# Windowed attention with sinks, then RWKV channel mix: the sink tokens' rows of v come by four small transfers instead of a selection matmul per sequence, with new engine choices, order and buffers

## The chip, the cores and the metric

The kernel runs on one core of one Trainium2 chip. The metric is the device time of one execution in microseconds (us); the figure for the kernel before is the median of 3 runs, 165.95 us (165.86 to 165.98). In the profile the engines are PE (matrix products), PEld (loading of PE's weights), DVE (VectorE), ACT (ScalarE), POOL (GpSimd) and SP (SyncE, which here only issues transfers). SPq, POOLq and the like are the instruction queues of these engines. "L676" is line 676 of the kernel before; in the kernel after, the same code stands 10 to 13 lines further down (L808 is L819 there, L939 is L950, and so on).

## The reference

Two layers follow each other. The first is attention in which each position sees the 4 first positions of its sequence (the sinks) and the last 128 positions. B = 4 sequences, H = 8 heads, S = 768 positions, D = 64:

```python
scores = scale * np.matmul(q, k.transpose(0, 1, 3, 2))
keep = is_sink | in_window            # pos < 4, or 0 <= i - j < 128
a = softmax(where(keep, scores, -1e9))
x = matmul(a, v)                      # then heads side by side: [B, S, 512]
```

The second is the RWKV channel mix over the 512 columns of x, with 1024 hidden columns:

```python
xk = mu_k * x + (1.0 - mu_k) * x_prev      # x_prev: one position earlier
xr = mu_r * x + (1.0 - mu_r) * x_prev
k = np.maximum(xk @ w_k, 0.0)
out = sigmoid(xr @ w_r) * (k * k @ w_v)
```

All inputs and the output are fp32; the kernel computes its products in bf16.

## The kernel before, in words

**Tiling.** The work is cut into 12 units: 4 sequences of 3 blocks with 256 positions each, unit u being block u mod 3 of sequence u div 3. A unit passes through four functions, and PE works on several units at a time.

- `prepare` loads q, k and v of the unit on SP (fp32), casts them to bf16 (L536 or L543 for q and k, L646 for v) and turns q and k so that the head dimension lies on the partitions. Where PE does this, it takes four transposes into a PSUM bank (L576) and a copy out (L589). For k of units 4 to 11 and q of units 8 to 11 SP issues DMA transposes instead (L562); such a transpose stands in SP's queue between loads and stores.
- `attend` computes the transposed scores (L721), their exponential (ACT, L775), the mask (DVE, L789; units 0 and 1 get it as a bias from products with an identity, L728), and the products with v (L808). A column of ones beside v gives the sum of the weights, so L822 takes its reciprocal and L825 multiplies. For the blocks 1 and 2 of a sequence the sinks are outside the window's blocks: their scores are products of `ksink` and q (L696), exponentiated (L703), and their share of the result is the product with `vsink` (L763).
- `mix` brings x into the layout with columns on the partitions (PE L849 with a copy L858; for units 9 to 11 DMA transposes from SP, L869), then DVE makes the difference td to the previous position (L877) and from it xk and xr (L888, four instructions of half a unit's width each).
- `ffn` runs one unit behind: the key products (L939, 32 per unit, xk by w_k), relu (L949 on ACT, L953 on DVE), square (L963 on DVE, L967 on ACT), the gate's products (L979, xr by w_r) and tanh (L985), the value products (L997), the final product with the gate (L1006) and the store (L1013). The last half of the last unit is done in two parts (`last_product`, L909, L919, L924).

**The sinks' operands.** Once per sequence, from its first block. `ksink` holds for each pair of heads c a group of 32 columns, in which head a of the pair has its four sinks' keys at columns 4a to 4a + 3; the rest is zero. Two copies on POOL fill it from kt (L670). `vsink` has the matching rows: partition 32c + 4a + i holds row i of v for head 2c + a, in this head's columns and nowhere else. To get rows 0 to 3 of v to these partitions, PE multiplies the bf16 v of the block with `spread`, a 0/1 matrix that picks them (L676, 512 columns into a bank), and DVE multiplies the bank by the 0/1 matrix `hmask` into `vsink` (L680). There are two `ksink` and two `vsink`, used by turns.

**What sets the order.** The whole program is written as a list of operations (`P.op`), each with an engine, a cost for a planner, what it reads and writes, and the pool from which it takes a buffer. The finished plan stands in the file as three tables: `CHOICE` gives the engine of operations that may run on several (casts, copies, relu, square), `SLOTS` the buffer that each operation takes, `ORDER` the sequence in which the operations are emitted. Each engine executes its instructions in that order, and waits at an instruction until the results it needs are there and its buffer is free. A negative number in `ORDER` is a fill: a product with zeros into a bank (L1018), during the start. Within POOL's and SP's queues transfers are issued in the same way, in order. PSUM has 8 banks: two pairs for scores (`sc`) and four for all else (`bank`); the operand bank of L676 is one of these four.

The constants are made by POOL at the start: `ident` and `hmask` (L418), `spread` (L451), the masks, and the column of ones of `vsink` (L470).

## Time and profile before

| | |
|---|---|
| median of 3 runs | 165.95 us (165.86 to 165.98) |
| span of the profiled execution | 164.3 us, so 1.65 us below the median |
| PE busy | 158.4 us (96%), 1603 matmuls |
| DVE busy | 145.4 us (89%), 381 instructions |
| ACT busy | 131.2 us (80%), 218 instructions |
| POOL busy | 13.5 us (8%), 38 instructions |
| data moved | 34.6 MB, 211 GB/s on average |

The span runs from the first to the last record of the profiled execution; a run's time also has what lies around it. A row of the timeline has its start, its length, its engine, its line and operation, the tile written and the tile read, and the number of instructions that follow each other; in square brackets stand the idle time of the engine before it and what ended that. The chain of waits is followed back from the last instruction: each row is what the next one waited for, or the instruction before it on the same engine. A row of the windows has the stretch, its length, and then for PE, weight loads, DVE, ACT and POOL the busy time with the number of instructions, PE's granted clock (1.00 is the full one), the share of the time in which DMA engines moved data, and GB/s. A row that groups instructions has their number, their busy time and mean length in ns, and the idle time before them with what ended it; the row of a tile has the shortest, median and longest length in ns and the first and last start.

### The profile page before, as it was taken

How to read it: one execution, taken by the hardware profiler on the slowest of the kernel's cores; microseconds unless marked ns; L12 is line 12 of the kernel's file. 1: busy time of each engine (PE TensorE's matmuls, PEld its weight loads, DVE VectorE, ACT ScalarE, POOL GpSimd, SP SyncE). 2: the span in 40 equal slices, each digit the busy share in tenths (PEclk: the TensorE clock that was granted, in tenths of full speed). 3: DMA queues.
4: the chain of work that ended last, by engine and by line, in shares of the span. 5: the costliest groups of instructions: out<-in, count | busy, mean ns of one | idle time of the engine just before them, and what ended most of it. 6: DMA issues, size and time to landing. Idle time of an engine off the chain costs nothing.

```text
span 164.3 us, 4195 instructions
## 1 busy us (share of the span) xinstructions
PE 158.4 (96%) x1603; PEld 102.6 (62%) x1603; DVE 145.4 (89%) x381; ACT 131.2 (80%) x218; POOL 13.5 (8%) x38
## 2 busy tenths in 40 slices
PE   6999889999999999999999999999999999999992
PEld 2455568866467587577566775856575765664851
DVE  5259999999999999989999999999999999789752
ACT  3277999999999999999999999997668759163240
POOL 6409300010000000060000000000000000000000
PEclk9999999999999999999999999999999999999999
DMA  4999999999969896999999887986996955077743
GB/s 120 247 305 311 348 335 355 301 354 210 228 154 270 135 240 148 234 198 167 224 216 157 188 156 163 235 146 150 199 123 136 362 149 200 0 90 297 262 185 128
DMA packets 79042, 34.60 MB, mean 211 GB/s; under 512 B 67112, under 2 KB 73520, under 8 KB 79024
## 3 DMA queue, kind: packets, MB, share of 16 engines
q1 hardware_dynamic: 79008, 34.35, 86.3%
q8 instruction: 12, 0.20, 0.6%
q14 instruction: 6, 0.05, 0.1%
q10 hardware_dynamic: 16, 0.00, 0.0%
HBM read 24.12 MB, written 6.29 MB: 185 GB/s over the span
## 4 chain that ended last, share of the span: by engine, by line
PE 79%; ACT 8%; SPq 4%; DMA 3%; issue 2%; DVE 1%; POOL 1%; DVEq 0%; ACTq 0%; POOLq 0%
PE bank L997 23%; PE bank L939 23%; PE bank L979 12%; PE bank L808 6%; PE sc L721 6%; SPq L337 3%; DMA qs<-in_q_dram 3%; PE bank L576 2%; ACT e L775 2%; PE bank L849 2%; ACT rl L949 1%; PE bank L763 1%; ACT qt L589 1%; PE bank L909 1%; PE bank L1018 1%
## 5 line engine op out<-in xcount | busy, mean ns | idle before, releaser
L775 ACT ACTIVATE e<-sc 128x1024 bf16<-128x1024 f32 (+1 forms) x48 | 46.1, 994 | 1.8 <-PE sc L721 1.7
L939 PE MATMUL bank<-xk,wk_sb 128*128 128x256 bf16 x384 | 47.1, 273 | 0.0
L997 PE MATMUL bank<-wv_h,kk 128*128 128x512 bf16 x184 | 43.1, 379 | 0.1
L939 PEld LDWEIGHTS <-wk_sb 128*128 128x128 bf16 x384 | 36.4, 98 | 7.4 <-issue 0.4
L949 ACT ACTIVATE rl<-bank 128x512 bf16<-128x512 f32 x40 | 24.2, 625 | 8.6 <-PE bank L939 7.1
L997 PEld LDWEIGHTS <-kk 128*128 128x128 bf16 x184 | 17.1, 98 | 17.8 <-issue 0.4
L789 DVE TENSOR_TENSOR e<-e,mask 128x1024 bf16<-128x1024 bf16 (+1 forms) x40 | 25.4, 642 | 0.7 <-ACT e L775 0.5
L979 PE MATMUL bank<-wr_sb,xr 128*128 128x512 bf16 x96 | 23.7, 379 | 0.0
L888 DVE SCALAR_TENSOR_TENSOR xk<-td,mu_all,xt 128x256 bf16<-128x256 bf16 x48 | 22.4, 483 | 0.3
L888 DVE SCALAR_TENSOR_TENSOR xr<-td,mu_all,xt 128x256 bf16<-128x256 bf16 x48 | 22.1, 475 | 0.2
L967 ACT ACTIVATE kk<-rl 128x512 bf16<-128x512 bf16 x29 | 18.3, 664 | 4.2 <-DVE rl L953 4.0
L985 ACT ACTIVATE th<-bank 128x512 f32<-128x512 f32 x24 | 15.1, 646 | 5.7 <-PE bank L979 5.7
L825 DVE TENSOR_TENSOR x<-bank,rec 128x256 bf16<-128x256 f32 x48 | 19.2, 416 | 0.4
L808 PE MATMUL bank<-vb,e 128*128 128x65 bf16 x352 | 16.6, 194 | 0.0
L1006 DVE SCALAR_TENSOR_TENSOR w<-th,bank 128x512 f32<-128x512 f32 x19 | 13.0, 682 | 3.6 <-issue 1.8
L808 PEld LDWEIGHTS <-e 128*128 128x128 bf16 x352 | 13.6, 97 | 3.5
L979 PEld LDWEIGHTS <-xr 128*128 128x128 bf16 x96 | 8.8, 98 | 8.6 <-issue 0.2
L721 PE MATMUL sc<-qt,kt 64*128 64x128 bf16 (+1 forms) x256 | 13.9, 238 | 0.0
L721 PEld LDWEIGHTS <-kt 64*128 64x128 bf16 x256 | 8.9, 94 | 5.7 <-issue 3.1
L1018 PE MATMUL bank<-warm 128*128 128x512 bf16 x30 | 10.6, 484 | 1.1 <-DVE warm L1038 1.1
L877 DVE TENSOR_TENSOR td<-xt 128x512 bf16<-128x512 bf16 x24 | 10.3, 428 | 0.7 <-ACT xt L858 0.5
L589 ACT COPY qt<-bank 128x512 bf16<-128x512 bf16 x15 | 9.4, 643 | 1.0 <-PE bank L576 1.0
(74 smaller groups left out, 161.7 us busy)
## 6 DMA issues: line engine op xcount, KB each, us to landing
ks<-in_k_dram SPq DMA_DIRECT2D x24, 256.0 KB, 4.7
qs<-in_q_dram SPq DMA_DIRECT2D x24, 256.0 KB, 4.4
vs<-in_v_dram SPq DMA_DIRECT2D x24, 256.0 KB, 4.4
out_dram<-w SPq DMA_DIRECT2D x19, 256.0 KB, 2.7
w<-in_moe_w_k_dram SPq DMA_DIRECT2D x2, 1024.0 KB, 10.4
w<-in_moe_w_v_dram SPq DMA_DIRECT2D x2, 1024.0 KB, 9.3
w<-in_moe_w_r_dram SPq DMA_DIRECT2D x1, 1024.0 KB, 9.7
out_dram<-ob SPq DMA_DIRECT2D x4, 256.0 KB, 2.6
```

Source lines behind the costliest of these rows:

```text
L721: nc.tensor.matmul(out=sc[:, a, o0:o1], lhsT=lhs[rows], rhs=rhs[rows], start=u not in BIAS, stop=True, skip_group_check=u in BIAS)
L775: nc.scalar.activation(out=buf[ek][:, :, lo:], in_=buf[sck][:, :, lo:], func=AF.Exp, scale=scale)
L789: nc.vector.tensor_tensor(out=at, in0=at, in1=m, op=ALU.mult)
L808: nc.tensor.matmul(out=o[:, g, a, :], lhsT=e[:, a, e0:e0 + 128], rhs=rhs, start=(T == 0 and i == 0), stop=(i == len(blocks) - 1), skip_gro ...
L825: P.op("DVE", dve(256), lambda ok=ok, rk=rk, c=c: nc.vector.tensor_tensor(out=buf["x", u][:, :, 128 * c:128 * c + 128].rearrange("p g (a d ...
L888: nc.vector.scalar_tensor_tensor(out=buf[key][:, c, :], in0=buf[tk][:, i, :], scalar=mu[w][:, c:c + 1], in1=xt[:, c, t0 - 1:t0 + 255], op0 ...
L939: nc.tensor.matmul(out=ps[:, i, :], lhsT=wk_sb[:, c, 128 * f:128 * f + 128], rhs=xk[:, c, :], start=(c == 0), stop=(c == NC - 1), skip_gro ...
L949: nc.scalar.activation(out=buf[rk], in_=buf[psk].rearrange("p (i t) -> p i t", i=2), func=AF.Relu)
L967: nc.scalar.activation(out=buf["kk", u][:, 2 * f2:2 * f2 + 2, :], in_=buf[rk], func=AF.Square)
L979: nc.tensor.matmul(out=buf[psk], lhsT=buf["xr", u][:, c, 128 * g:128 * g + 128], rhs=wr_sb[:, c, :], start=(c == 0), stop=(c == NC - 1))
L985: P.op("ACT", act(512), lambda psk=psk, tk=tk: nc.scalar.activation(out=buf[tk], in_=buf[psk], func=AF.Tanh, scale=0.5), rank + 4 + g, tak ...
L997: nc.tensor.matmul(out=buf[psk], rhs=wv_h[:, f, :], lhsT=buf["kk", u][:, f, 128 * g:128 * g + 128], start=(f == 0), stop=(f == NF - 1))
```

## The change

**The sinks' rows of v.** A new fp32 tile `vstage` [128, 4, 64] is cleared with the other zeros. Four transfers issued by POOL (L491 of the kernel after) fill its partitions i, 16 + i, 32 + i, ... (one of each 16) with row i of v: partition 16h + i gets row i of head h, for all four sequences. The sinks of head h therefore stand at 16h to 16h + 3 rather than at 32c + 4a; the copies into `ksink` (L680 after) and `hmask` are moved to the same places. `vsink` of a sequence is then one product, `vstage` of that sequence (the same for all eight heads) by `hmask` (L686 after). It reads no bank, and may stand on POOL or DVE. The selection matmul, its bank, `spread` and its constants are gone.

```diff
@@ tiles and constants
-    spread = tile1([128, 128], BF16, "spread")
+    vstage = tile1([128, B, D], FP32, "vstage")
...
-        for t, value in ((ones, 1.0), (spread, 0.0), (hmask, 1.0)):
+        for t, value in ((ones, 1.0), (hmask, 1.0)):
...
-        for t in ksink + vsink:
+        for t in ksink + vsink + [vstage]:
             nc.vector.memset(t, 0.0)
...
-    def make_spread():
-        for a in range(2):
-            nc.gpsimd.tensor_copy(
-                out=spread[0:NS, :].rearrange("p (c w) -> p c w", w=32)[:, :, 4 * a:4 * a + NS],
-                in_=ident[0:NS, 0:NS].unsqueeze(1).to_broadcast([NS, NP, NS]))
...
-            keep(m, -4 * a, [[-32, NP], [0, D + 1]], 1, m)
-            keep(m, 3 + 4 * a, [[32, NP], [0, D + 1]], -1, m)
+            keep(m, -16 * a, [[-32, NP], [0, D + 1]], 1, m)
+            keep(m, 3 + 16 * a, [[32, NP], [0, D + 1]], -1, m)
...
+    for i in range(NS):
+        P.op("POOL", 1000.0, lambda i=i: nc.gpsimd.dma_start(
+            out=vstage[i::16], in_=v[:, :, i, :].rearrange("b h d -> h b d")), -50,
+            service=60.0, descs=32, reads=["stage0"], writes=[("vstage", i)])
@@ prepare
-                nc.gpsimd.tensor_copy(out=kz[rows, :, 4 * a:4 * a + NS],
+                nc.gpsimd.tensor_copy(out=kz[rows, :, 16 * a:16 * a + NS],
                                       in_=first(rows))
...
-        psk = ("vsp", b)
-        P.op("PE", 220.0, lambda: nc.tensor.matmul(
-            out=buf[psk].rearrange("p (h d) -> p h d", h=H), lhsT=spread,
-            rhs=buf["vb", u][:, 0, :, 0:D], start=True, stop=True), rank + 4, lag=PE_LAG,
-            take=[("bank", psk)], hold=[("vb", u)], reads=["spread", ("vb", u, 0)], writes=[psk])
-        P.op("DVE", dve(512), lambda: nc.vector.tensor_tensor(
-            out=vsink[b % 2][:, :, 0:D], op=ALU.mult, in1=hmask[:, :, 0:D],
-            in0=buf[psk].rearrange("p (h d) -> p h d", h=H)), rank + 4, hold=[psk],
-            reads=[psk, "hmask", "sinks"], writes=[("vsink", b % 2)])
+        def sink_values(engine):
+            return lambda: engine.tensor_tensor(
+                out=vsink[b % 2][:, :, 0:D], op=ALU.mult, in1=hmask[:, :, 0:D],
+                in0=vstage[:, b, :].unsqueeze(1).to_broadcast([128, H, D]))
+
+        P.op("POOL", 1250.0, sink_values(nc.gpsimd), rank + 4, port=True,
+             alts={"POOL": (1250.0, sink_values(nc.gpsimd), True),
+                   "DVE": (dve(512), sink_values(nc.vector), True)},
+             reads=[("vstage", i) for i in range(NS)] + ["hmask", "sinks"],
+             writes=[("vsink", b % 2)])
```

**The tables.** `CHOICE`, `ORDER` and `SLOTS` are new throughout (the first line of each table of choices shows how they read):

```diff
 CHOICE = {
-    92: "ACT", 93: "ACT", 94: "ACT", 95: "ACT", 97: "ACT", 100: "ACT", 102: "DVE", 105: "DVE",
...
+    95: "DVE", 96: "DVE", 97: "ACT", 98: "ACT", 99: "DVE", 100: "ACT", 101: "DVE", 102: "DVE",
...
```

What this does to the number of instructions: PE has four matmuls fewer and 29 fills rather than 30. DVE's program has 11 instructions fewer: 12 casts of q, k and v, three of the four products into `vsink` and two copies into xt are gone from it; two casts of w_k, one copy into kt, two relus, one square and a memset of `vstage` are new, and `spread`'s memset is gone. ACT has five fewer: two casts of w_k, one of q, k and v, a copy into kt, two relus and a square are gone, two copies into xt are new. POOL has 61 rather than 43: 16 casts of q, k and v instead of 3, three products into `vsink`, the four transfers. SP issues as many transfers as before; it loads both halves of q of unit 0 first and then k, and q of unit 1 ahead of v of unit 0.

Three places show how the order moved. On PE, in the middle of the program, the block in which the second sequence's selection matmul stands (x_107 is a unit's attention result on its way into its transpose, ksink the sinks' keys). Before:

```order
L939 LDWEIGHTS wk_sb
L939 MATMUL bank_63<-xk_115,wk_sb 128x256
L676 LDWEIGHTS spread
L676 MATMUL bank_64<-vb_138,spread 128x512
L979 LDWEIGHTS xr_119
L979 MATMUL bank_66<-wr_sb,xr_119 128x512
...
L849 MATMUL bank_63<-ident,x_107 128x128
L849 LDWEIGHTS x_107
...
L696 MATMUL bank_64<-qt_89,ksink_152 32x256
L696 LDWEIGHTS ksink_152
```

After, around the transpose of the same unit:

```order
L860 MATMUL bank_66<-ident,x_107 128x128
L860 LDWEIGHTS x_107
...
L732 MATMUL sc_62<-qt_89,kt_88 128x128
L732 LDWEIGHTS kt_88
...
L707 MATMUL bank_64<-qt_89,ksink_151 32x256
L707 LDWEIGHTS ksink_151
...
L1008 MATMUL bank_65<-wv_h,kk_120 128x512
L1008 LDWEIGHTS kk_120
```

The selection matmul is gone from between the key products and the gate's; the sinks' scores stand directly behind the first group of scores, where before key products, the gate's and a second group of scores came in between.

On POOL, from the first sequence's keys of the sinks to the end of the program. Before:

```order
L470 COPY vsink_153<-hmask 128x8
L470 COPY vsink_154<-hmask 128x8
L670 COPY ksink_151<-kt_85 64x4x4 x2
L418 AFFINE_SELECT mask_147<-ones 128x128 x3
L434 MEMSET mask_147 4x256
L670 COPY ksink_152<-kt_88 64x4x4 x2
L670 COPY ksink_151<-kt_87 64x4x4 x2
L670 COPY ksink_152<-kt_86 64x4x4 x2
```

After (up to the last rows, which are two more casts of q, a product into vsink, the last copies into ksink and a cast of v):

```order
L680 COPY ksink_150<-kt_85 64x4x4 x2
L656 CAST vb_136<-vs_74 128x8x64 x2
L686 TENSOR_TENSOR vsink_153<-vstage,hmask 128x8x64
L553 CAST kb_79<-ks_67 128x2x4x64
L680 COPY ksink_151<-kt_88 64x4x4 x2
L686 TENSOR_TENSOR vsink_152<-vstage,hmask 128x8x64
L546 CAST kb_81<-ks_69 128x512
L546 CAST kb_79<-ks_67 128x512
L680 COPY ksink_150<-kt_87 64x4x4 x2
L546 CAST kb_79<-ks_67 128x512 x2
L546 CAST qb_83<-qs_70 128x512 x2
L546 CAST kb_80<-ks_69 128x512
```

POOL's queue held only the copies into ksink after the start; now casts of kb, qb and vb stand between them. The casts with 128x512 elements (L546) feed the DMA transposes of SP.

On DVE, from the last attention results (x_109, that of unit 11) to the last xk (xk_116, also of unit 11). Before:

```order
L825 TENSOR_TENSOR x_109<-bank_64,rec_105 128x2x128
L1006 SCALAR_TENSOR_TENSOR w_77<-th_130,bank_66 128x512
L822 RECIPROCAL rec_106<-bank_65 128x4
L825 TENSOR_TENSOR x_109<-bank_65,rec_106 128x2x128
...
L877 TENSOR_TENSOR td_111<-xt_156 128x512
L888 SCALAR_TENSOR_TENSOR xk_116<-td_111,mu_all,xt_156 128x256 x2
L877 TENSOR_TENSOR td_110<-xt_156 128x512
L888 SCALAR_TENSOR_TENSOR xr_119<-td_111,mu_all,xt_156 128x256
L888 SCALAR_TENSOR_TENSOR xr_119<-td_110,mu_all,xt_156 128x256
L888 SCALAR_TENSOR_TENSOR xk_116<-td_110,mu_all,xt_156 128x256
L888 SCALAR_TENSOR_TENSOR xr_119<-td_110,mu_all,xt_156 128x256
L888 SCALAR_TENSOR_TENSOR xk_116<-td_110,mu_all,xt_156 128x256
```

After:

```order
L836 TENSOR_TENSOR x_109<-bank_66,rec_106 128x2x128
L836 TENSOR_TENSOR x_109<-bank_63,rec_105 128x2x128
L888 TENSOR_TENSOR td_110<-xt_156 128x512
...
L888 TENSOR_TENSOR td_112<-xt_156 128x512
L899 SCALAR_TENSOR_TENSOR xr_119<-td_112,mu_all,xt_156 128x256
L899 SCALAR_TENSOR_TENSOR xk_116<-td_112,mu_all,xt_156 128x256
L888 TENSOR_TENSOR td_111<-xt_156 128x512
L899 SCALAR_TENSOR_TENSOR xk_116<-td_111,mu_all,xt_156 128x256
L899 SCALAR_TENSOR_TENSOR xk_116<-td_112,mu_all,xt_156 128x256
L899 SCALAR_TENSOR_TENSOR xk_116<-td_111,mu_all,xt_156 128x256
```

The product with the gate (L1006) between the last two attention results is gone from there, and of the four xr instructions of unit 11 one rather than three stands ahead of the last xk.

46 lines of the change are left out of this document (30 added, 16 removed), and 157 rows, old and new, of tables (ORDER, SLOTS).

## The prediction

> **What bounds the kernel now.** I read three views first: the page's busy shares, the busy time of each engine by stretch (cut where the chain of waits changes its character), and the chain itself in order of time.
>
> ```profile
> span 164.3 us, 4195 instructions
> ...
> PE 158.4 (96%) x1603; PEld 102.6 (62%) x1603; DVE 145.4 (89%) x381; ACT 131.2 (80%) x218; POOL 13.5 (8%) x38
> ...
> PE 79%; ACT 8%; SPq 4%; DMA 3%; issue 2%; DVE 1%; POOL 1%; DVEq 0%; ACTq 0%; POOLq 0%
> ```
>
> The chain that ended last is PE for 79% of the span; nothing else holds a tenth of it. POOL is nearly empty, and that is where the change puts work.
>
> ```profile
> 0.00:24.13 24.13, 21.61 (x218) 11.81 (x219) 16.88 (x55) 16.44 (x26) 9.86 (x32) 1.00 0.94 277
> 24.13:140.50 116.37, 116.22 (x1253) 77.81 (x1252) 112.94 (x294) 107.16 (x180) 3.62 (x6) 1.00 0.93 206
> 140.50:161.10 20.60, 20.60 (x136) 13.01 (x133) 15.15 (x34) 7.59 (x13) 0.00 (x0) 1.00 0.54 168
> ```
>
> The columns are PE, weight loads, DVE, ACT, POOL, PE's granted clock, DMA share, GB/s. Up to 24.13 the first key product has not begun: this is the start, set by loads and by DVE and ACT. From there to 140.50 attention and FFN run mixed; PE is full, but DVE has only 116.37 - 112.94 = 3.43 us free. After 140.50 PE works off products alone, and both others have time.
>
> **The removed matmul.**
>
> ```profile
> 16.93 0.23 PE bank L676
> ...
> 17.43 0.59 DVE vsink L680
> ...
> 18.06 0.40 PE bank L576 x4
> ...
> 24.13 0.90 PE bank L939 x8
> ...
> 51.95 0.22 PE bank L676
> ...
> 121.75 0.22 PE bank L676
> ```
>
> L676's record is longer, but a place on PE costs 0.22 from start to start. Three of the four lie in the stretch where PE is the chain (the third, near 68.5, is taken as the others): 3 x 0.22 = 0.66 us less. The fourth, at 16.93, lies in the start; it and L680 hold a bank for which PE waits until 18.06, but what the start waits for at its end is the first key product's data, so I count it at nothing there. Bounds of this term: 0 (PE only waits longer elsewhere) and 0.88.
>
> **What leaves DVE and ACT.** The duration of a record is longer than its place, since records overlap:
>
> ```profile
> 70.25 0.42 DVE L646 CAST vb<-vs 128x512 bf16<-128x512 f32 x1
> 70.59 0.42 DVE L543 CAST qb<-qs 128x512 bf16<-128x512 f32 x1
> 70.93 0.41 DVE L963 TENSOR_TENSOR kk<-rl 128x512 bf16<-128x512 bf16 x1
> 71.26 1.28 DVE L789 TENSOR_TENSOR e<-e,mask 128x1024 bf16<-128x1024 bf16 x2
> ...
> 64.45 0.68 ACT L536 CAST kb<-ks 128x512 bf16<-128x512 f32 x1
> 64.96 1.10 ACT L775 ACTIVATE e<-sc 128x1024 bf16<-128x1024 f32 x1
> ```
>
> A cast takes 0.34 us of DVE and 0.51 of ACT. DVE's program loses 12 casts (12 x 0.34 = 4.1), three of four sink products (3 x 0.59 = 1.8) and two copies of xt (0.7). It gains two casts of wk, a kt copy, two relus (five at about 0.6, their records being near L680's) and one square (0.34). Net -3.2 us. ACT loses two casts of wk, one other cast, a kt copy, two relus and a square and gains two xt copies:
>
> ```profile
> L501 ACT ACTIVATE wk_sb<-w 128x1024 bf16<-128x1024 f32 x4 | 4.2, 1092 | 0.0
> L680 DVE TENSOR_TENSOR vsink<-bank,hmask 128x512 bf16<-128x512 f32 x4 | 2.7, 678 | 0.2 <-PE bank L676 0.2
> L543 POOL CAST kb<-ks 128x512 bf16<-128x512 f32 x2 | 1.4, 702 | 0.0
> L543 POOL CAST qb<-qs 128x512 bf16<-128x512 f32 x1 | 0.9, 865 | 6.7 <-DMA qs<-in_q_dram 6.7
> ```
>
> 2 x 0.95 + 3 x 0.5 = 3.4 us. Neither is on the chain for long. Where ACT is, its casts stand in it:
>
> ```profile
> 64.64 0.50 ACT kb L536
> ...
> 66.06 0.50 ACT vb L646
> ...
> 71.91 0.61 ACT kb L536
> ```
>
> These are three pieces of a run on ACT from 59.8 to 73.1 beside which PE goes on working. The gain there is between 0 (other ACT rows step into the place) and 1.6 (all three go). ACT shrinks by 3.4 in 107, or 3%; 3% of 13.3 is 0.4, and DVE, which stands at 97% and also shrinks by 3%, I give 0.2. I take **-0.6**.
>
> **What POOL gets.** Thirteen more casts at 0.70 to 0.87, three sink products, and the issue of four small transfers. No row shows a two-input product on POOL; the nearest is the slowest cast of that size, 0.87, and from above the longest POOL record here, 2.30 (below). I take 0.87. The issue is not shown on POOL either: from below it cannot be under nothing, from above 2.30 again; SP's issue of an ordinary load, 0.61 in the chain of waits (last of the rows below), is the nearest, and I take it. All of this, some 9 + 2.6 + 2.4 us, lies on an engine whose queue was idle for 6.7 us before its q cast (the L543 row) and almost always after 24, so its own time costs nothing. Two things can bring it onto the path.
>
> First, POOL and DVE hold each other up:
>
> ```profile
> 13.48 0.62 POOL L543 CAST kb<-ks 128x512 bf16<-128x512 f32 x1
> ...
> 13.75 0.62 DVE L877 TENSOR_TENSOR td<-xt 128x512 bf16<-128x512 bf16 x1
> ...
> L877 DVE TENSOR_TENSOR td<-xt x24: 389/420/621, 13.8 to 149.1; 128x512 bf16<-128x512 bf16 x24
> ...
> 32.55 0.79 POOL L670 COPY ksink<-kt 64x16 bf16<-64x16 bf16 x2 [14.55 <-ACT kt L589]
> 70.30 2.54 POOL L670 COPY ksink<-kt 64x16 bf16<-64x16 bf16 x2 [36.96 <-DMA kt<-kb]
> 96.30 0.45 POOL L670 COPY ksink<-kt 64x16 bf16<-64x16 bf16 x2 [23.47 <-DMA kt<-kb]
> ...
> L670 POOL COPY ksink<-kt x8: 188/196/2303, 16.2 to 96.6; 64x16 bf16<-64x16 bf16 x8
> ...
> 1.61 0.61 SPq L337
> ```
>
> A POOL cast cost the td beside it 0.62 - 0.42 = 0.20. Eleven of the casts and three products fall behind 24.13: 14 x 0.20 = 2.8 us of DVE, bounds 0 and, if every one stops DVE for its whole 0.87, 12. DVE's free 3.4 and its saved 3.2 cover the 2.8, so I count **0**; gone is this cover from 0.47 each upward. The other way, a copy of 0.19 took 2.30 at 70.30: it ended at 72.60, when DVE's unbroken row of casts and two-input products ended (71.26 + 1.28 = 72.54).
>
> The Trainium skill has a rule for it (SBUF — State Buffer, section "SBUF: two separate sides"): the pair of ports that VectorE and GpSimd share is an exclusive lock, held for a whole instruction by whoever starts first. The trace agrees that one waits, but not for one instruction: POOL sat out six. By the rule alone a cast would wait for no more than the one instruction in front of it, 0.34 to 0.64 here, and the slower rival below would be worth less; the sum itself, which has this at 0, stays.
>
> Second, nine of the casts stand ahead of DMA transposes on SP, whose queue is in order: a late cast holds the loads behind it, and the scores that need its kt.
>
> **Start and end.** The first key product needs xk of unit 0, unit 0's two halves of q and k, and v. The new order loads q first and brings in q of unit 1 before v. ACT has 0.2 us more in front of its first wk cast (one exp for a cast and es), DVE about 0.5 more in front of the last xk; one group of scores (0.55) that stood behind the first key product now stands ahead. I take 0, with -0.5 to +1.5. At the end:
>
> ```profile
> 139.88 0.40 PE L808 MATMUL bank<-vb,e 128*128 128x65 bf16 x8
> ...
> 142.79 3.65 SPq L869 DMA_TRANSPOSE xt<-x  x2
> ...
> 147.88 0.42 DVE L877 TENSOR_TENSOR td<-xt 128x512 bf16<-128x512 bf16 x1
> ...
> 151.06 0.48 DVE L888 SCALAR_TENSOR_TENSOR xk<-td,mu_all,xt 128x256 bf16<-128x256 bf16 x1
> ...
> 152.25 3.66 PE L939 MATMUL bank<-xk,wk_sb 128*128 128x256 bf16 x32
> ```
>
> From the last attention product (139.88) to the last xk (151.54) pass 11.7 us; PE has other products until 152.25, 0.7 more. The new order leaves only 24 value matmuls, 32 key matmuls and 4 of the gate in between: 24 x 0.22 + 3.5 + 0.9 = 9.6 us after the group's own 0.24. DVE is quicker there: no L1006 ahead of x (0.6), and two xr fewer ahead of the last xk (0.8), so 11.7 - 0.2 - 1.4 = 10.1. A wait of 0.5 would be left; since td at 147.88 stood behind another DVE row and not surely behind the transfer, I take **+0.3** (0 to 0.8).
>
> **The sum.** -0.66 - 0.6 + 0 + 0.3 = -0.96 us. On the profiled span that is 164.3 to 163.3; the runs' median stands 165.95 - 164.3 = 1.65 above the span (start and end around it), which I keep: **165.0 us**. Own range of this case 164.4 to 165.6, all faster. A difference of 0.2% (0.33 us) is about what a measurement here can tell. Chance 0.42.
>
> **Rivals.**
> - Late casts on POOL: slower. For: the trace has POOL late by 2.1 us at 70.30, and the units' transposes have little room: those of unit 6 are issued at 66.22 and its scores run at 71.73. Against: the pairs at 32.55 and 96.30 took 0.79 and 0.45 where twice the median is 0.39: late by 0.4 and 0.1. The mean of three is 0.9. Four units (5, 6, 8, 10) have a kb cast on POOL; if 0.9 reaches PE in each, +3.6 on the sum, 168.6; at half, 166.8. It decides from 0.25 us of lateness per unit upward. I give a point between, 167.4, chance 0.22.
>
> ```profile
> 66.22 2.95 SPq L562 DMA_TRANSPOSE kt<-kb  x2
> ...
> 71.73 0.50 PE L721 MATMUL sc<-qt,kt 64*128 64x256 bf16 x8
> ```
>
> - The start is late: POOL's first queue now holds two q casts, four issues, hmask, bias1, then the casts of v for units 0 and 1. At 0.61 an issue it has some 3 us to spare before unit 1's v has landed; at 1.5 each that is used up, at 2.3 it is 3 us late in front of the attention of unit 1, of which half may hide: 166.5. Chance 0.12.
> - DVE and ACT are what spoils PE's stretch, and all of ACT's 3.4 comes off: -0.66 - 3.4 + 0.3, 162.2. For: DVE's 97%. Against: the chain has PE there, not DVE. Chance 0.10.
> - It does nothing: another wait takes each freed place, because each engine's order is fixed and all three are above 90%: 165.95, within 0.2%. Chance 0.14.
>
> So faster 0.42 + 0.10 = 0.52, same 0.14, slower 0.34. The range 163.2 to 167.4 leaves out the far half of the late casts and most of the largest gain.
>
> **What would show it.** Right: no L676, PE's matmuls 5 fewer (4 and one fill), the first L950 near 24, DVE's busy time near 142 to 145 and ACT's near 128, POOL's casts (L546, L553, L656) mostly under 1.2 us, the four L491 issues done before 14 us, the last key products starting some 10 us after the last attention product with a wait under 1 us. Wrong: POOL casts of 2 us and more with SP's transposes waiting for POOL and scores waiting for them (late casts); vb<-vs on POOL later than 21 us (late start); DVE records of td, xk, xr well over 0.5 in the middle. What would upset it all is an in-order wait of more than 1 us on PE at a place that the trace before has no row for.

## The result, and the profile after

The changed kernel takes **168.38 us** (median of 4 runs, 167.6 to 169.22); the kernel before took 165.96 beside it (165.86 to 166.21). The ratio is 1.0142, 95% interval 1.0106 to 1.0179: 1.4% or 2.4 us slower. The prediction was 165.0 us with a range of 163.2 to 167.4, so both the sign and the range were missed.

The changed kernel's page:

```profile
span 165.9 us, 4209 instructions
...
PE 157.6 (95%) x1598; PEld 101.3 (61%) x1598; DVE 144.7 (87%) x370; ACT 128.7 (78%) x213; POOL 26.9 (16%) x56
...
PE 72%; DVE 9%; SPq 7%; DMA 4%; ACT 3%; issue 3%; POOL 1%; DVEq 0%
```

What the prediction said of the work itself came out: five matmuls fewer on PE, DVE at 144.7, ACT at 128.7 us. But the chain of waits is now PE for 72%, no longer 79%, and DVE stands in it with 9% instead of 1%. PE's busy time is 0.8 us less and the span 1.6 us more, so PE idles 2.4 us more. The busy time by stretches tells where. First the kernel before (PE, weight loads, DVE, ACT, POOL, clock, DMA share, GB/s):

```profile
0.00:30.00 30.00, 27.48 (x282) 16.80 (x283) 22.65 (x69) 22.31 (x34) 9.86 (x32) 1.00 0.97 289
30.00:140.00 110.00, 109.85 (x1183) 72.49 (x1182) 106.67 (x278) 101.29 (x172) 3.62 (x6) 1.00 0.92 200
140.00:164.30 24.30, 21.11 (x145) 13.34 (x142) 16.07 (x36) 7.59 (x13) 0.00 (x0) 0.99 0.51 163
```

Then the changed kernel:

```profile
0.00:30.00 30.00, 25.37 (x268) 14.62 (x269) 22.71 (x64) 20.30 (x31) 14.31 (x38) 1.00 1.01 285
30.00:140.00 110.00, 109.60 (x1189) 72.75 (x1188) 105.57 (x270) 100.70 (x170) 12.59 (x18) 1.00 0.93 194
140.00:165.90 25.90, 22.67 (x149) 13.95 (x144) 16.46 (x38) 7.67 (x14) 0.00 (x0) 1.00 0.52 186
```

PE's idle time is 2.52 us in the first 30 us before and 4.63 after; in the middle 0.15 and 0.40; behind 140 us 3.19 and 3.23. So 2.1 of these 2.4 us of idle time arise **in the start**. The middle, where the prediction looked for gains and for the risk, loses a quarter of a microsecond, and the end nothing. (The profiled execution is the fastest of the four runs, 167.6 us; most of what the others lose beyond it is told in the last section.)

The end of the start on PE, in order of time. The first row is the first key product of the kernel before, the others are the changed kernel:

```profile
23.98 1.05 PE L939 MATMUL bank<-xk,wk_sb 128*128 128x256 bf16 x8
...
23.91 0.29 PE L774 MATMUL bank<-vsink,es 64*128 64x130 bf16 x4 [1.07 <-DVE x L836]
...
25.58 1.24 PE L1029 MATMUL bank<-warm 128*128 128x512 bf16 x5
26.71 0.40 PE L860 MATMUL bank<-ident,x 128*128 128x128 bf16 x4
26.95 1.04 PE L950 MATMUL bank<-xk,wk_sb 128*128 128x256 bf16 x8
```

The first key product (L950) stands at 26.95, where before it stood at 23.98 (the 24.13 of the chain of waits is where the row ahead of it ends). The `es` product (L774) had waited 1.07 us for DVE's x (L836), and the fills and the transposes (L860) came behind it. What DVE did until then:

```profile
18.64 0.41 DVE L553 CAST qb<-qs 128x512 bf16<-128x512 f32 x1
19.52 0.80 DVE L686 TENSOR_TENSOR vsink<-vstage,hmask 128x512 bf16<-128x512 f32 x1 [0.47 <-POOL vb L656]
20.24 0.51 DVE L888 TENSOR_TENSOR td<-xt 128x512 bf16<-128x512 bf16 x1
20.67 1.85 DVE L899 SCALAR_TENSOR_TENSOR xk<-td,mu_all,xt 128x256 bf16<-128x256 bf16 x2
22.44 0.87 DVE L899 SCALAR_TENSOR_TENSOR xr<-td,mu_all,xt 128x256 bf16<-128x256 bf16 x2
```

The single `vsink` product that the choice leaves on DVE (19.52) waits 0.47 us, and all of td, xk and xr stand behind it in DVE's order. The two xk at 20.67 take 1.85 us; the two xr behind them 0.87, the normal price. From 19.53 to 33.76 us the chain of waits of this kernel runs through DVE alone. POOL in the same time:

```profile
13.39 0.61 POOL L656 CAST vb<-vs 128x512 bf16<-128x512 f32 x1 [3.30 <-DMA vs<-in_v_dram]
13.94 0.54 POOL L491 DMA_DIRECT2D vstage<-in_v_dram  x1
...
17.79 0.66 POOL L656 CAST vb<-vs 128x512 bf16<-128x512 f32 x1 [2.60 <-DMA vs<-in_v_dram]
18.70 0.83 POOL L656 CAST vb<-vs 128x512 bf16<-128x512 f32 x1 [0.25 <-DMA vs<-in_v_dram]
19.48 1.41 POOL L431 TENSOR_SCALAR_AFFINE_SELECT mask<-ones 128x128 bf16<-128x128 bf16 x3
20.85 0.30 POOL L447 MEMSET mask<- 4x256 bf16 x1
21.12 1.11 POOL L686 TENSOR_TENSOR vsink<-vstage,hmask 128x512 bf16<-128x512 f32 x1
```

Two things follow from these rows. The fourth small transfer (the issue at 13.94) stands in POOL's queue behind a cast of v that waited 3.30 us for its load. Its semaphore event reaches DVE at 19.4, and that is what the product at 19.52 waited for; the row puts the wait down to the last `vb` cast, which ended at 19.53, but the like row of a second run of this kernel (below) names the transfer. And POOL's product of the second sequence, 21.12 to 22.23, runs beside the second xk, which takes about a microsecond more than the first.

The groups of POOL over the whole kernel (busy time, mean length in ns, idle time before):

```profile
L686 POOL TENSOR_TENSOR vsink<-vstage,hmask 128x512 bf16<-128x512 f32 x3 | 3.8, 1266 | 0.1
...
L546 POOL CAST kb<-ks 128x512 bf16<-128x512 f32 x5 | 3.1, 615 | 33.2 <-DMA ks<-in_k_dram 31.9 <-DVE e L800 1.2
...
L491 POOL DMA_DIRECT2D vstage<-in_v_dram x4 | 2.5, 628 | 0.4 <-DVE vstage L421 0.4
```

The five casts of this row take 0.62 us in the mean and POOL's other groups of casts 0.60 to 0.70, less than the 0.70 to 0.87 that were taken from before; the product takes 1.27 on average rather than 0.87; a transfer costs POOL 0.63 to issue, as estimated.

### The profile page after: what moved, and what is told of

Its sections match the earlier page's. It is cut to its first block, busy times and chain, and to the rows that moved or that the text cites. A ratio compares the mean times of both kernels' runs of the same rounds, so it can differ in the third digit from the quotient of the medians.

```text
span 165.9 us, 4209 instructions
## 1 busy us (share of the span) xinstructions
PE 157.6 (95%) x1598; PEld 101.3 (61%) x1598; DVE 144.7 (87%) x370; ACT 128.7 (78%) x213; POOL 26.9 (16%) x56
## 4 chain that ended last, share of the span: by engine, by line
PE 72%; DVE 9%; SPq 7%; DMA 4%; ACT 3%; issue 3%; POOL 1%; DVEq 0%
PE bank L1008 23%; PE bank L950 22%; PE bank L990 10%; PE bank L819 6%; SPq L349 5%; PE sc L732 5%; DMA vs<-in_v_dram 4%; PE bank L860 2%; DVE xk L899 2%; DVE td L888 1%; SPq L319 1%; DVE xr L899 1%; PE bank L774 1%; PE bank L586 1%; PE bank L920 1%
## 5 line engine op out<-in xcount | busy, mean ns | idle before, releaser
L786 ACT ACTIVATE e<-sc 128x1024 bf16<-128x1024 f32 (+1 forms) x48 | 45.6, 971 | 4.0 <-PE sc L732 3.7
L950 PE MATMUL bank<-xk,wk_sb 128*128 128x256 bf16 x384 | 47.9, 273 | 0.0
L1008 PE MATMUL bank<-wv_h,kk 128*128 128x512 bf16 x184 | 44.3, 379 | 0.3 <-DVE wv_h L515 0.3
L950 PEld LDWEIGHTS <-wk_sb 128*128 128x128 bf16 x384 | 36.0, 98 | 6.4 <-issue 0.3
L960 ACT ACTIVATE rl<-bank 128x512 bf16<-128x512 f32 x38 | 22.2, 605 | 10.6 <-PE bank L950 10.2
L899 DVE SCALAR_TENSOR_TENSOR xk<-td,mu_all,xt 128x256 bf16<-128x256 bf16 x48 | 23.6, 512 | 0.1
L899 DVE SCALAR_TENSOR_TENSOR xr<-td,mu_all,xt 128x256 bf16<-128x256 bf16 x48 | 22.8, 486 | 0.1
L996 ACT ACTIVATE th<-bank 128x512 f32<-128x512 f32 x24 | 14.1, 603 | 9.7 <-PE bank L990 9.7
L836 DVE TENSOR_TENSOR x<-bank,rec 128x256 bf16<-128x256 f32 x48 | 19.7, 416 | 0.5
L978 ACT ACTIVATE kk<-rl 128x512 bf16<-128x512 bf16 x28 | 17.5, 636 | 0.1
L819 PE MATMUL bank<-vb,e 128*128 128x65 bf16 x352 | 16.0, 194 | 0.2
L1029 PE MATMUL bank<-warm 128*128 128x512 bf16 x29 | 9.3, 457 | 1.3 <-DVE warm L1049 1.1
```

Of the source, the lines that this page charges most:

```text
L786: nc.scalar.activation(out=buf[ek][:, :, lo:], in_=buf[sck][:, :, lo:], func=AF.Exp, scale=scale)
L819: nc.tensor.matmul(out=o[:, g, a, :], lhsT=e[:, a, e0:e0 + 128], rhs=rhs, start=(T == 0 and i == 0), stop=(i == len(blocks) - 1), skip_gro ...
L836: P.op("DVE", dve(256), lambda ok=ok, rk=rk, c=c: nc.vector.tensor_tensor(out=buf["x", u][:, :, 128 * c:128 * c + 128].rearrange("p g (a d ...
L899: nc.vector.scalar_tensor_tensor(out=buf[key][:, c, :], in0=buf[tk][:, i, :], scalar=mu[w][:, c:c + 1], in1=xt[:, c, t0 - 1:t0 + 255], op0 ...
L950: nc.tensor.matmul(out=ps[:, i, :], lhsT=wk_sb[:, c, 128 * f:128 * f + 128], rhs=xk[:, c, :], start=(c == 0), stop=(c == NC - 1), skip_gro ...
L960: nc.scalar.activation(out=buf[rk], in_=buf[psk].rearrange("p (i t) -> p i t", i=2), func=AF.Relu)
```

## The experiments

All ratios are to the kernel before, run on the same chip, whose medians were 166.2 to 166.3 us in these sessions; intervals are 95%. Points are hundredths of that time, 1.66 us each. ORDER and CHOICE are the tables of the changed kernel unless another is named; where a diff shows a part of a table, the rest is only shifted.

**The changed kernel once more** (e0), and **the change of the path alone** (e1): the order, choices and buffers of the kernel before, with the four transfers in place of `spread`'s copies in POOL's queue, L676 gone, and the product on DVE where it was.

> The changed kernel once more, beside the others. Its four runs so far spread from 167.6 to 169.22 us, where those of before lie within 0.35. If the spread is a matter of the chip, five rounds narrow it to one value near 168; if it is the kernel's own (a start that depends on when a transfer lands), the spans go on differing by 1 us and more. Ratio to before 1.010 to 1.018 either way.

> The kernel before, in its own order, with only the sinks' operand path of the change: vstage filled by the four transfers (all four issued at the place where spread was made), vsink by a product of vstage and hmask on DVE, no selection matmul. Theory 'the new order is to blame': the path alone gives the forecast term back, 3 x 0.22 to 4 x 0.22 = 0.66 to 0.88 us less, 165.1 to 165.3 us. Rival 'the transfers themselves disturb the start': 166.5 us or more, with a later first key product. Rival 'freed PE time is filled by another wait': 165.9.

```diff
@@ before.py (e1; with vstage cleared and hmask at 16a, as in the change)
     def make_spread():
-        for a in range(2):
-            nc.gpsimd.tensor_copy(...)
+        for i in range(NS):
+            nc.gpsimd.dma_start(out=vstage[i::16], in_=v[:, :, i, :].rearrange("b h d -> h b d"))
...
-        P.op("PE", 220.0, lambda: nc.tensor.matmul(...
+        P.op("PE", 220.0, lambda: None, rank + 4, lag=PE_LAG,
...
-            in0=buf[psk].rearrange("p (h d) -> p h d", h=H)), rank + 4, hold=[psk],
+            in0=vstage[:, b, :].unsqueeze(1).to_broadcast([128, H, D])), rank + 4, hold=[psk],
```

The first gave 1.0143 (1.0111 to 1.0175), median 169.02 us. The second gave 0.9982 (0.9963 to 1.0001), 166.14 us. The transfers in place of the matmul are therefore not what costs; they save 0.3 us, with an interval from nothing to 0.6. The loss comes with the new order, choices and the products on POOL.

The second run of the changed kernel has its first product on DVE with the releaser named:

```profile
19.76 0.69 DVE L686 TENSOR_TENSOR vsink<-vstage,hmask 128x512 bf16<-128x512 f32 x1 [0.25 <-DMA vstage<-in_v_dram]
```

**Its waits in the start, one by one.** In the first of three runs (e2) the fourth transfer (92) is issued right behind the third (89). In the second (e3) the fourth transfer stays where it was; the first sequence's mask (85) is made behind the third transfer, and the second sequence's product (290) stays on POOL but goes behind the third sequence's copies into `ksink` (289), to 41 us. The third (e5) leaves all of these and puts four fills into PE's gap.

> The changed kernel with the fourth transfer issued straight behind the third on POOL, ahead of the cast of v of unit 0 that waits 3.3 us for its load. In the profile of after, DVE stood from 19.05 to 19.43 us at the first product into vsink until that transfer had landed (19.40). Theory 'late fourth transfer': that wait goes, 0.4 us less than the changed kernel in the profiled run, more in its slower runs, and the spread of its runs shrinks to a few tenths. Rival 'POOL's work beside DVE and the order are what costs': 0 to 0.2 us less, the same spread.

> The changed kernel with two pieces of POOL's work moved out of the stretch from 19.5 to 22.2 us: mask0 made behind the third transfer, the second sequence's product into vsink behind its ksink copies. In that stretch one xk took 1.42 us instead of 0.47, beside that product. Theory 'POOL holds DVE up while DVE is behind': xk back at 0.48 us, the first key product 1.0 to 1.3 us earlier, 0.8 to 1.2 us less than the changed kernel. Rival 'the order puts the first key products late whatever DVE does': under 0.3 us less.

> The changed kernel with four more fills on PE in the gap from 22.84 to 23.91 us, ahead of the second sink values of unit 1; no data is made sooner. In the repeat of the changed kernel PE's granted clock fell to 0.5 from 25.84 for 3.41 us, and five of its six runs show a mean clock of 0.99. Theory 'the gap on PE makes the clock fall': all runs at a mean clock of 0.997 to 1.0, median 0.8 to 1.4 us below the repeat's, span near 166. Rival 'the clock falls for another reason': the same 0.99 in most runs and the same median.

```diff
@@ ORDER (e2)
-    86, 89, 147, 148, 17, 150, 143, 18, 118, 137, -2, -4, 124, 138, 133, 128, 19, 20, 92, 87, 119,
+    86, 89, 92, 147, 148, 17, 150, 143, 18, 118, 137, -2, -4, 124, 138, 133, 128, 19, 20, 87, 119,
@@ ORDER (e3)
-    86, 89, 147,
+    86, 89, 85, 147,
...
-    209, 192, 85, 258,
+    209, 192, 258,
...
-    275, 290, 15,
+    275, 15,
...
-    289, 381,
+    289, 290, 381,
@@ ORDER (e5)
-    165, 184,
+    165, -2, -2, -2, -2, 184,
```

They gave 1.0118 (1.0086 to 1.0150), 1.0104 (1.0079 to 1.0128) and 1.0112 (1.0082 to 1.0142). Each is 0.25 to 0.4 points below the changed kernel, none clearly so, since the intervals overlap; no single wait of the start carries the loss. Part of the difference is the granted clock, which the last section tells of: it fell in two of e2's six runs and in none of e3's and e5's.

In e3 the two xk of the start take 0.87 us rather than 1.85, and the first key product comes 0.7 us earlier, at 26.24. But PE then waits elsewhere, for wv_h from DVE, where the changed kernel waits 0.29 us. PE, POOL and DVE in e3:

```profile
45.34 1.89 PE L1008 MATMUL bank<-wv_h,kk 128*128 128x512 bf16 x8 [1.16 <-DVE wv_h L515]
...
41.28 2.40 POOL L686 TENSOR_TENSOR vsink<-vstage,hmask 128x512 bf16<-128x512 f32 x2
...
41.61 1.07 DVE L888 TENSOR_TENSOR td<-xt 128x512 bf16<-128x512 bf16 x1
42.61 1.34 DVE L899 SCALAR_TENSOR_TENSOR xk<-td,mu_all,xt 128x256 bf16<-128x256 bf16 x1
```

Beside the two products td and xk take 1.07 and 1.34 us instead of 0.42 and 0.47, and wv_h stands behind them. The product's cost has moved with the product.

**PE's order in the start.** The theory was that the key products need only xk, while x of the next unit, its transpose and the five fills stand ahead of them for nothing. In the first run (e4) xk goes ahead of xr on DVE, the first key products go ahead of the `es` products on PE, and the fills are gone; two banks are exchanged for it. The second (e6) has the moves of e2 and e3 as well.

> The changed kernel with the first key products moved ahead of the second transpose of unit 1 on PE, the five fills between them left out, the last two xk of unit 0 ahead of its last two xr on DVE, and the two banks of the moved operations exchanged. Theory 'the order sets the late start': the first key product comes 1.2 to 1.5 us earlier (25.5 instead of 26.95 us), the kernel 0.8 to 1.4 us faster than the changed kernel. Rival 'POOL beside DVE': DVE is still behind, PE only waits at the next place instead, under 0.4 us.

> The changed kernel with the edits of the three start kernels together: fourth transfer behind the third, mask0 behind that, the second sequence's product into vsink behind its ksink copies, and the order with the first key products early. If the late start is the whole of the loss and these are its causes, the first key product comes near 24.8 us and the kernel takes 165.7 to 166.5 us where before takes 166.3. If the middle loses too (more POOL work beside DVE), it stays 1 us or more above before.

```diff
@@ ORDER (e4; 165, 159: xk; 167, 168: xr; 233, 234: first key products)
-    166, 167, 168, 170,
+    166, 165, 159, 170,
...
-    201, 165, 184, 253, 190, 98, 181, 207, 26, 186, 249, 159, 191, 208,
-    187, 209, 192, 85, 258, 188, 210, 212, 211, 23, -4, -4, -4, -4, -2, 214, 233, 234, 263, 95,
+    201, 184, 253, 190, 98, 181, 207, 26, 186, 249, 191, 208, 233, 234,
+    187, 209, 192, 85, 258, 188, 167, 168, 210, 212, 211, 23, 214, 263, 95,
```

They gave 1.0202 (1.0175 to 1.0228) and 1.0192 (1.0164 to 1.0220): certainly no faster than the changed kernel, and by their ratios slower, against the theory. The clock fell in four of the first's six runs and in one of the second's, so it is not the reason for both. PE in the first of them:

```profile
25.53 1.03 PE L950 MATMUL bank<-xk,wk_sb 128*128 128x256 bf16 x8 [0.41 <-DVE xt L869]
...
29.24 4.90 PE L950 MATMUL bank<-xk,wk_sb 128*128 128x256 bf16 x28 [1.64 <-DVE wk_sb L517]
```

The first key products came at 25.53, as meant; the next ones, 3.7 us later, waited 1.64 us for a cast of w_k on DVE, which stood behind everything that had been held up. DVE is short of time in the start, and an order on PE that asks for its results earlier only moves the wait.

**The products on DVE.** Here the three products of the sequences 1 to 3 go back to DVE in the new order. The next adds the early transfer and the early mask. The third of the set adds ACT in place of DVE for the two casts of w_k; the fourth moves the second sequence's product on DVE from 32 to some 40 us.

> The changed kernel with the three products into vsink that stood on POOL made by DVE, in the same places of the order. Theory 'a product on POOL costs DVE as much as it takes there (0.65 to 0.95 us seen at 21.1 and 42.6)': DVE neither gains nor loses by it, the start gains 0.95 us and loses 0.6 later: 0.2 to 0.8 us less than the changed kernel. Rival 'POOL's products are free': 3 x 0.6 us more on DVE, 0.3 to 1.5 us more.

> The changed kernel with everything taken away that POOL does beside DVE from 19.0 to 22.5 us: products into vsink on DVE, fourth transfer behind the third, mask0 behind that. Theory 'DVE is what the start waits for, and POOL's work and the transfer delay it': 0.2 to 0.6 us less than with the products on DVE alone (ratio to before 1.0079 there), so 1.004 to 1.007, first key product 25.5 to 26.0 us. Rival 'what is left of the late start is the order and DVE's own work': 1.007 to 1.009.

> As the kernel with DVE cleared, and the two casts of w_k that the change moved to DVE (27.76 and 28.70 us, 0.60 each) made by ACT, as before. Theory 'DVE's added work in the start costs': DVE is 1.2 us ahead behind 27.8 us, 0.4 to 1.0 us less. Rival 'ACT is as full': its exponentials come 1.9 us later and nothing is won, or up to 1 us is lost.

> The changed kernel with DVE cleared (ratio 1.0042), and the second sequence's product into vsink on DVE moved from 32.0 us behind its ksink copies (some 40 us), where PE does not wait for it: PE stood 0.68 us at 33.1 behind it. Theory 'the rest of the loss sits at the edge of DVE's start': 0.3 to 0.7 us less, ratio 1.000 to 1.003. Rival 'the wait only moves': 1.004.

```diff
@@ CHOICE (e7; e8, e9 and e15 too)
-    290: "POOL", 528: "POOL", 762: "POOL",
+    290: "DVE", 528: "DVE", 762: "DVE",
@@ ORDER (e8, e9, e15)
-    86, 89, 147,
+    86, 89, 92, 85, 147,
@@ CHOICE (e9)
-    95: "DVE", 96: "DVE",
+    95: "ACT", 96: "ACT",
@@ ORDER (e15)
-    275, 290, 15,
+    275, 15,
...
-    289, 381,
+    289, 290, 381,
```

| run | ratio | median, us |
|---|---|---|
| e7, products on DVE | 1.0079 (1.0058 to 1.0100) | 167.60 |
| e8, and transfer and mask early | 1.0042 (1.0023 to 1.0061) | 167.06 |
| e9, and w_k cast on ACT | 1.0128 (1.0089 to 1.0168) | 168.52 |
| e15, as e8 with one product later | 1.0046 (1.0025 to 1.0066) | 167.32 |

Taking the three products off POOL gives back 0.64 points of the 1.43, although DVE then has three instructions more: the opposite of what busy times would say. (Part of the 0.64 is the clock, told in the last section: against e5, in which it does not fall, e7 is lower by 0.33, with overlapping intervals.) With POOL's products out of the way, the early transfer and mask are worth another 0.37, whose intervals just touch. ACT has no room for the casts of w_k either. In e8 the first key products start 1.7 us after those of the kernel before (25.66 and 23.98). PE waits three times from 20 to 34 us: 0.55 and 0.40 us for ACT's exponentials (es and e), as in the changed kernel, and the wait in the second row:

```profile
25.66 1.04 PE L950 MATMUL bank<-xk,wk_sb 128*128 128x256 bf16 x8
...
33.10 0.52 PE L819 MATMUL bank<-vb,e 128*128 128x65 bf16 x12 [0.68 <-DVE vb L656]
```

That `vb` cast stands behind the product on DVE; moving the product (e15) removes this wait and changes nothing in the time. Where the wait went is not shown; e15's profile lacks 17 of PE's matmuls. What is left of the loss, 0.42 points, or 0.60 against the path alone in the old order, is seen best in one stretch. First e8, then the kernel before:

```profile
20.00:34.00 14.00, 12.23 (x163) 9.40 (x164) 13.90 (x37) 13.68 (x22) 2.04 (x1) 1.00 1.10 352
```

```profile
20.00:34.00 14.00, 13.50 (x191) 10.89 (x188) 13.72 (x37) 14.00 (x22) 0.74 (x2) 1.00 1.10 338
```

PE is busy 12.23 of 14 us there rather than 13.50. This stretch is not the whole account, since PE is busy 12.89 us of it in e15, which is no faster. Which of the new order's moves in the start does it, no run tells: none moves ACT's exponentials, or puts SP's loads back into the order they had.

**The products on POOL in the old order.** To price them apart from the new order, the same product goes to POOL in e1: for the sequences 1 to 3, for the second sequence alone (19 us, in the start), and for the last two alone (39 and 98 us).

> The kernel in its old order with the new operand path (ratio to before 0.9982), and the products into vsink of the sequences 1 to 3 on POOL instead of DVE. Theory 'a product on POOL stops DVE for most of its 1.1 us': DVE saves 3 x 0.6 and loses up to 3 x 0.95, the time stays within 0.3 us of the same kernel with products on DVE or gets longer. Rival 'POOL's time is free': DVE has 1.8 us less to do in its fullest stretch, 0.2 to 0.6 us less.

> The old order with the new operand path, and only the second sequence's product into vsink on POOL, which there falls at 19.1 us, in the start. With three products on POOL the kernel stood at 1.0073, with none at 0.9982: 1.5 us. Theory 'it is the product in the start': most of it, 0.8 to 1.2 us, ratio 1.003 to 1.006. Rival 'each product costs the same': 0.5 us, 1.001.

> The counterpart: only the products of the third and fourth sequence on POOL (39.9 and 98.8 us). Theory 'it is the product in the start': 0.3 to 0.6 us, ratio 1.000 to 1.002. Rival 'each product costs the same': 1.0 us, 1.004.

```diff
@@ e1_old_order (e10; in e13 "if b == 1", in e14 "if b > 1")
-        P.op("DVE", dve(512), lambda: nc.vector.tensor_tensor(
+        P.op("DVE", dve(512), lambda: (nc.gpsimd if b else nc.vector).tensor_tensor(
```

They gave 1.0073 (1.0047 to 1.0099), 1.0043 (1.0020 to 1.0067) and 1.0037 (1.0015 to 1.0059), where e1 is at 0.9982: three products cost 0.91 points or **1.5 us**, the one in the start 1.0, the two later 0.9. The rows show what happens beside a product. In e1 DVE has in the start:

```profile
18.43 0.43 DVE L542 CAST qb<-qs 128x512 bf16<-128x512 f32 x1
18.79 0.47 DVE L885 SCALAR_TENSOR_TENSOR xr<-td,mu_all,xt 128x256 bf16<-128x256 bf16 x1
```

In e13 POOL has its product and DVE the same two instructions:

```profile
19.09 1.11 POOL L677 TENSOR_TENSOR vsink<-vstage,hmask 128x512 bf16<-128x512 f32 x1
```

```profile
18.97 1.52 DVE L542 CAST qb<-qs 128x512 bf16<-128x512 f32 x1
20.41 0.47 DVE L885 SCALAR_TENSOR_TENSOR xr<-td,mu_all,xt 128x256 bf16<-128x256 bf16 x1
```

The cast of q takes 1.52 us instead of 0.43, 1.09 more: it was held for about the 1.11 us that the product takes, and ended 0.29 us after it. Later in the program it is the same. In e14 on POOL, and then on DVE:

```profile
39.17 1.48 POOL L677 TENSOR_TENSOR vsink<-vstage,hmask 128x512 bf16<-128x512 f32 x1 [5.39 <-issue]
...
98.23 1.12 POOL L677 TENSOR_TENSOR vsink<-vstage,hmask 128x512 bf16<-128x512 f32 x1
```

```profile
39.68 1.25 DVE L874 TENSOR_TENSOR td<-xt 128x512 bf16<-128x512 bf16 x1
...
98.49 1.14 DVE L885 SCALAR_TENSOR_TENSOR xk<-td,mu_all,xt 128x256 bf16<-128x256 bf16 x1
```

These DVE instructions stand at 0.42 and 0.47 undisturbed, so 0.83 and 0.67 were lost. With the 1.09 of e13 that is 2.6 us of DVE for three products, against 3 x 0.6 us that DVE saves: a net of 0.8. How this becomes 1.5 us of the kernel's time is not shown row by row.

**The casts on POOL in the old order.** The prediction's slower rival was that casts on POOL come too late, its gain that DVE and ACT lose them. Nine casts of the second half, those of k and q for units 5 to 11 that the changed kernel also has on POOL, go there: once in the kernel before, once in e1.

> The kernel before with nine casts of k and q (units 5, 6, 8, 9, 10, 11) on POOL, as the change has them, and nothing else. The prediction's rival 'late casts on POOL': each of them waits behind DVE's unbroken work, the DMA transposes and scores behind them wait too, 0.9 to 3.6 us more. The prediction's own term: 9 x 0.2 us of DVE, covered by its free time, and seven casts less on ACT: 0 to 0.6 us less.

> The kernel in its old order with the new operand path (products into vsink on DVE) and the nine casts of k and q on POOL: the two parts that each came out at or below before, together. If they add up: 0.9982 x 0.9962 = 0.9944 of before, 0.9 us less. Rival 'both give back the same time once': 0.996 to 0.998.

```diff
@@ CHOICE of before.py (e11) and of e1_old_order (e12)
-    439: "DVE", 906: "DVE", 910: "DVE",
+    439: "POOL", 519: "POOL", 673: "POOL", 677: "POOL", 753: "POOL",
+    757: "POOL", 828: "POOL", 906: "POOL", 910: "POOL",
```

They gave 0.9962 (0.9939 to 0.9985), 165.89 us, and 0.9961 (0.9938 to 0.9984), 165.50 us. The casts make the kernel **faster**, by 0.6 us (0.25 to 1.0). Both of these kernels beat the one before and the changed one, and with the casts on POOL, taking the matmul away too adds nothing that can be told apart. A cast of the first on POOL, and the DVE instruction beside it:

```profile
60.77 0.61 POOL L542 CAST kb<-ks 128x512 bf16<-128x512 f32 x1 [9.28 <-DVE e L795]
...
87.20 0.61 POOL L542 CAST qb<-qs 128x512 bf16<-128x512 f32 x1 [10.53 <-PE bank L945]
```

```profile
60.85 0.80 DVE L883 TENSOR_TENSOR td<-xt 128x512 bf16<-128x512 bf16 x1 [0.26 <-ACT xt L864]
...
87.25 0.84 DVE L894 SCALAR_TENSOR_TENSOR xk<-td,mu_all,xt 128x256 bf16<-128x256 bf16 x1
```

The td takes 0.80 instead of 0.42 and the xk 0.84 instead of 0.47: a cast of 0.61 us costs DVE some 0.4 here, and gives back the 0.34 or 0.51 us of its own place on DVE or ACT. Three of the nine came from DVE and six from ACT. On e11's page DVE is busy for 146.0 us instead of 145.4, and ACT for 129.0 instead of 131.2: what the casts gave back is ACT's time, not DVE's. The products came off DVE alone and had nothing of the kind to give.

## Why the prediction was wrong

**The step that failed** is the pair "No row shows a two-input product on POOL ... I take 0.87" and "I count 0". What POOL costs DVE was priced at 0.20 us a piece, from one row, in which td met a cast that had already run for 0.27 us; and it was covered by DVE's free time averaged over 24 to 140 us.

In place of that price the runs show this: a DVE instruction on tiles in SBUF (td, xk, a cast) that meets a running POOL instruction ends 0.27 to 0.29 us after it. It is so in all seven pairs of rows: the product at 21.12 in the changed kernel (it ends at 22.23, the second xk at 22.52), the three of e13 and e14, the two casts of e11 and the cast in the prediction's own row (14.10 and 14.37). A cast and a product hold DVE in the same way. DVE loses nearly all that is left of POOL's instruction, which is 0.61 us for such a cast and 1.11 to 1.5 us for a product. The three products of e13 and e14 took 0.67 to 1.09 us from DVE, and three products cost 1.5 us (e10 against e1).

The cover was wrong too. The prediction had all three products behind 24.13; the first came at 21.12, in the start, where DVE has no spare time at all (its rows from 19.52 on follow each other without a gap, and PE waits at 23.91 for what it makes). An average over the stretch behind it could not pay for that. For casts the 0.20 came out, by luck: five of e11's nine held a DVE instruction, for 0.28 to 0.42 us, and four held none, 0.20 in the mean.

The Trainium skill states the rule on the page SBUF — State Buffer, section "SBUF: two separate sides": a GpSimd instruction and a VectorE instruction that has two SBUF inputs or runs in a two-port mode lock each other out, the later one waiting for the whole instruction. The trace agrees that DVE waits for POOL's whole instruction (the ends 0.27 to 0.29 us apart). It does not show that the earlier start wins: the cast of q that was held for 1.09 us in e13 has its start at 18.97, the product at 19.09. The prediction applied this rule to POOL waiting for DVE, and took the other way round, where it was expensive, from a single row. The page GPSIMD Engine Reference of the Trainium skill, section "4.1 Engine selection", puts two-input operations on GpSimd at about half VectorE's speed; the trace has 1.11 us at the least on POOL against 0.68 on DVE, a factor of 1.6.

**Point by point.**
- *The removed matmul, -0.66.* Right in sign perhaps, too large: with everything else held, it is -0.3 us (0 to 0.6), and nothing that shows on top of the casts. In e1's profile PE is busy 157.2 us, 1.2 less than before, and the span is 163.9, only 0.4 less: the rest came back as idle time.
- *Relief of DVE and ACT, -0.6.* The nine casts alone give the same size, -0.6 (e11), but they are a part of what the term counted, and all of it came from ACT, so the agreement is partly luck. In the changed kernel it is not to be seen: PE's idle time in the middle did not shrink but rose by 0.25 us, and a product on POOL stands beside the one wait that is left there (td at 42.55 takes 1.07 us, and PE waits 0.29 us for wv_h at 45.41).
- *Issues, 0.61 each at no cost.* Their length was right (0.63). Not counted was that the fourth stands behind a cast that waits for its load. The transfer and mask early are worth 0.37 points once the products are off POOL (e8 against e7).
- *Start, 0 (-0.5 to +1.5).* PE's idle time there rose by 2.1 us, beyond the upper bound. The bound came from instructions counted ahead of the first key product, and held none for a wait behind POOL.
- *End, +0.3.* Nothing: PE's idle time behind 140 us is 3.19 and 3.23.
- *Late casts* fall as a rival: casts on POOL make the kernel faster, and the changed kernel's take 0.60 to 0.70 us in the mean while PE's idle time in the middle rose by only 0.25 in all.
- *The late start* named the right place and the right queue, with the wrong mechanism. Its condition was not met (an issue took 0.63, not 1.5; the casts of v were done by 19.5, before the 21 us that were to show it), and its 166.5 was short.
- Of the signs that were to show the prediction wrong, two came: the DVE records of td, xk and xr "well over 0.5", from the second xk on, and the wait of more than 1 us on PE at a place without a row before (1.07 at 23.91).

In points, the loss of 1.43 takes apart so far: products off POOL 0.64 (about 0.3 of it the clock, by e5; told next), transfer and mask early 0.37, and 0.42 that stay with the new order, whose cause is open. These are differences between runs with intervals of about 0.2 to 0.3 each. So the products on POOL and the fall of the clock together are the largest part, but not half of the loss. The rest lies with the transfer, the mask and the order of the start, which the prediction took at 0.

## What to carry to other kernels

Where DVE is full, a two-input operation moved from DVE to POOL is not free even if POOL is empty: here the DVE instruction beside it ended only 0.28 us after it. Price it by its own length, at the place where it runs, and look first at the stage in which DVE has no gap. Casts were worth moving here, since they are half as long and most of them came from ACT; products were not. In POOL's queue a small transfer was issued only when the cast ahead of it had got its data, 3.30 us later, so small early transfers belong ahead of anything that waits for a load. A term that averages over a stage must not cover a cost that falls in another one.

## What was unexpected: the clock

The granted clock was no term of the prediction. In the profiled execution of the changed kernel run again, two stretches of 3.41 us around the end of the start are these:

```profile
22.43:25.84 3.41, 2.05 (x35) 1.43 (x35) 3.38 (x13) 3.41 (x5) 0.00 (x0) 1.00 1.15 310
25.84:29.25 3.41, 3.41 (x15) 1.89 (x14) 3.02 (x8) 1.52 (x4) 0.00 (x0) 0.50 1.15 315
```

After a stretch in which PE was busy for 2.05 of 3.41 us, with no gap longer than 1.15 us, the clock fell to half for the next 3.41 us. (The stretch before these two, busy for 2.50 us, was not followed by a fall.) There fills, transposes and the first key products took:

```profile
25.69 2.18 PE L1029 MATMUL bank<-warm 128*128 128x512 bf16 x5
27.66 0.64 PE L860 MATMUL bank<-ident,x 128*128 128x128 bf16 x4
28.09 1.61 PE L950 MATMUL bank<-xk,wk_sb 128*128 128x256 bf16 x8
```

This is 2.18 instead of 1.24 us, and 1.61 instead of 1.04. Five of the six runs of this kernel had a mean clock of 0.99 and spans of 167.0 to 167.7 us; the sixth, at 1.00, had 166.0. So the fall is worth 1 to 1.7 us when it comes, and it explains most of the spread from 167.6 to 169.4; the execution profiled first had none. With the four fills of e5, 0.22 us each, the clock stayed at 0.999 or more in all six runs, and with e7's and e8's products on DVE it did not fall either (0.997 or more), nor in e3 (0.997 or more). e5's median of 167.93 stands near the 167.77 of the one run above that had no fall: without it the change would cost some 0.9 to 1.1%, not 1.4. The page TensorE: Matmul & The Clock Gate of the Trainium skill (Part 1) has activity windows of 3413 ns: after an idle one the clock halves, after a busy one it comes back. The trace agrees in the length, 3.41 us; but the stretch before the fall was not idle, PE was busy for 60% of it.
